# First chunks in three transfers, chunk 1 by terms, last tile scaled by ScalarE

## The chip, the cores and the metric

The kernel runs on one core of a Trainium2 chip. The metric is device time in microseconds of one execution. Engines: TensorE (PE in the rows, its weight load PEld), VectorE (DVE), ScalarE (ACT), GpSimd (POOL) and SyncE (SP), which here only issues transfers.

## The reference

A gate mixes a linear-attention block and a dense block over the same 2048 x 448 input:

```python
qkv = x @ wqkv                       # 16 heads of 28
pq, pk = phi(q), phi(k)              # phi(t) = where(t > 0, t + 1, exp(t)) + 1e-6
kv = einsum("bhsd,bhse->bhde", pk, v); z = pk.sum over s
a = (pq @ kv) / (pq . z + 1e-6) @ wo
h = x @ w1 + b1                      # w1: 448 x 1792
b = relu(h)**2 @ w2 + b2             # w2: 1792 x 448
g = sigmoid((x * gate_w).sum(-1))
return g * a + (1 - g) * b
```

## The kernel before

Every float32 operand is split into a high part in float32r and a low remainder, so a product is three matmuls: high by high, high by low, low by high. ScalarE mostly makes the high parts (`split_hi`, line 63), VectorE the low ones (`split_lo`, line 71).

Tokens go in 4 blocks of 512 (`TB`), hidden features in 14 tiles of 128. The contraction over 448 input features is cut into 4 chunks c = 0 to 3 of 128 rows; chunk 3 holds 64 features twice, so that two matmuls do for it. `up_chunk` (line 218) issues one chunk's two or three terms of one hidden tile, and its argument `only` picks a single term. `hidden` applies bias, relu and square; `down` multiplies by w2 into four accumulators `o_ps`; `finish` (line 275) ends an output tile: `u = o_ps * (1 - g) + part`, where `part` holds what was summed earlier, and a transfer out.

The order on TensorE, VectorE and ScalarE is the order of the code. SyncE's and GpSimd's instructions are placed by a scheduler as early as their waits allow. SyncE's transfers go in turn over eight semaphores, so one also waits for the landing of the one eight places before. Buffers for short-lived data are 15 slots used in turn (`slot`, line 54); a tile that reuses a slot waits until the old one has been read.

The start (lines 173 to 206 and 537 to 560): 14 matmuls on constants run on TensorE (line 177) while the first transfers are on their way. The first two, `xwr`, each bring half the columns of chunk 0 of x beside half of chunk 0 of w1 (128 x 512, 256 KB each). Then come chunks 1 to 3 of x (`xr`) and w1 (`w1r`), 256 KB each, and later weights. For chunk 0 ScalarE makes x's high part and VectorE w1's, half by half. TensorE multiplies the first half of x for hidden tiles 0 and 1, then the second half (line 547), then hidden tiles 2 and 3 over all 512 columns, then the two terms with low parts. Chunks 1 to 3 go tile by tile: all terms of hidden tile 0, then of tile 1, and so on, into the four accumulators `first[0..3]` (`h_ps` in the rows).

The end (lines 765 to 774): the last token tile's result is finished in two column ranges, 0 to 256 and 256 to 448. VectorE does both, one after the other, from the same PSUM tile; SyncE sends out the first, ScalarE's queue the second.

Of the kernel before, what the change touches and what calls it, by code (L numbers as in the profile page):

```python
# [7 lines left out]
F = mybir.dt.float32  # L8
R = mybir.dt.float32r
AF = mybir.ActivationFunctionType  # L10
ALU = mybir.AluOpType
PSUM = bass.MemoryType.PSUM

S, D, FF, H = 2048, 448, 1792, 16
DH = D // H
P = 128
TB = 512
# [10 lines left out]


@with_exitstack  # L30
def gated_mix_kernel(ctx: ExitStack, tc: tile.TileContext, xw, xt, xn, wk, wq, wv, wo, w1a, w1b, w2, b1, b2, gw,
                     hmask, kvmask, halves, out):
    nc = tc.nc
    act, dve, pool, pe, sp = nc.scalar, nc.vector, nc.gpsimd, nc.tensor, nc.sync
# [13 lines left out]
    def bank(name):  # L48
        turn[0] ^= 1
        return ms_p.tile([P, 512], F, name=name, tag=f"ms{turn[0]}")  # L50
# [3 lines left out]
    def slot(shape, dt, name):  # L54
        return work.tile(shape, dt, name=name, tag="s", bufs=NSLOT)

    def load(dst, src):
        sp.dma_start(out=dst, in_=src)
# [4 lines left out]
    def split_hi(eng, hi, src):  # L63
        if eng is act:
            act.activation(hi, src, AF.Copy)  # L65
        elif eng is pool:
            pool.tensor_scalar(hi, src, 1.0, 0.0, op0=ALU.mult, op1=ALU.add)
        else:
            eng.tensor_copy(hi, src)  # L69

    def split_lo(eng, lo, src, hi):
        eng.tensor_tensor(lo, src, f32(hi), op=ALU.subtract)  # L72
# [100 lines left out]
    part = [keep.tile([P, D], F, name=f"part{t}") for t in range(NT)]  # L173
# [8 lines left out]
    dve.memset(side[64:], 1.0)  # L182

    xw_raw = []
    for n in range(2):
        xw_raw.append(slot([P, TB], F, f"xwr{n}"))
        load(xw_raw[n], xw[n])
    for c in range(1, 4):
        load_x(0, c)
        load_w1(0, 0, c)  # L190
# [27 lines left out]
    def up_chunk(ps, b, f, c, only=None):  # L218
        h, fl = divmod(f, NH)
        g, i = divmod(fl, 4)  # L220
        w, cols = w1_s[h, g], slice(i * P, (i + 1) * P)
        xh, xl = xs[b]
        if c < 3:
            terms = [(w[:, c, cols], xh[:, c]), (w[:, c, cols], xl[:, c]), (w[:, 4 + c, cols], xh[:, c])]
        else:
            terms = [(w[:, 3, cols], xh[:, 3]), (w[:, 3, cols], xl[:, 3])]
        for n, (a, m) in enumerate(terms):
            if only in (None, n):
                pe.matmul(ps, a, m, start=(c == 0 and n == 0), stop=(c == 3 and n == 1))  # L229
# [17 lines left out]
    o_ps = {}  # L247
# [24 lines left out]
        for i in range(4):  # L272
            dve.tensor_tensor(part[4 * b + i], o_ps[i][:, :D], b2_s, op=ALU.add)

    def finish(b, i, cols=slice(0, D), eng=sp):
        t = 4 * b + i
        u = slot([P, D], F, f"out{t}_{cols.start}")[:, cols]
        dve.scalar_tensor_tensor(u, o_ps[i][:, cols], gate[:, 1, t:t + 1], part[t][:, cols], op0=ALU.mult,  # L278
                                 op1=ALU.add)
        eng.dma_start(out=out[t * P:(t + 1) * P, cols], in_=u)  # L280


    pend = {}
# [250 lines left out]

    first = [mm_p.tile([P, 512], F, name=f"h_ps0_{f}", tag="mm") if f < 2 else bank(f"h_ps0_{f}") for f in range(4)]
    for c in range(4):
        if c == 0:
            xs[0] = new_x(0)  # L540
            w, (xh, xl) = new_w1(0, 0), [x[:, 0] for x in xs[0]]
            sides = slice(0, TB // 2), slice(TB // 2, TB)
            for n, cols in enumerate(sides):
                split_hi(act, xh[:, cols], xw_raw[n][:, sides[0]])
                split_hi(dve, w[:, 0, cols], xw_raw[n][:, sides[1]])
                for f in range(2):
                    pe.matmul(first[f][:, cols], w[:, 0, f * P:(f + 1) * P], xh[:, cols], start=(n == 0), stop=False)  # L547
            for m, (lo, hi) in enumerate(((xl, xh), (w[:, 4], w[:, 0]))):
                for n, cols in enumerate(sides):
                    split_lo(dve, lo[:, cols], xw_raw[n][:, sides[m]], hi[:, cols])  # L550
        else:
            split_x(0, c)
            split_w1(0, 0, c)
        if c == 0:
            for n in range(3):
                for f in range(0 if n else 2, 4):
                    up_chunk(first[f], 0, f, c, n)
        else:
            for f in range(4):
                up_chunk(first[f], 0, f, c)  # L560
    split_w2(0)
    split_w2(1)
    wk_s = keep.tile([P, 7, D], R, name="wk_s", tag="wkm", bufs=1)
# [53 lines left out]
    for b in range(1, NB):  # L617
        for f in range(NH):
            leave = leaves[b][f]
            run_todo()  # L620
            up(b, f)
            if f == 0:
                down(b - 1, NH - 1)
                half_done(b - 1)
                if b == 1:
                    for c in range(1, 4):
                        todo += gram(0, c)
                        run_todo()
            else:
                down(b, f - 1, leave=leave)  # L630
            if f == 1:
                todo += late_keys
                run_todo()
            if f == 0:
                load_xn(4 * b)
            if f < 4:
                if f < 3:
                    load_xn(4 * b + f + 1)
                if f == 0 and leave:
                    late_keys = keys(4 * b, leave)  # L640
                else:
                    late_keys = []
                    todo += keys(4 * b + f)
            elif f < 6:
                todo += gram(b, f - 4)
            else:
                todo += gram(b, 2)
                run_todo()
                todo += gram(b, 3)
            if b + 1 < NB:  # L650
                if 1 <= f < 5:
                    load_x(b + 1, f - 1)
                if 3 <= f:
                    split_x(b + 1, f - 3)
            if b == 2:
                if f < 4:
                    load_wq(f)
                if 1 <= f < 5:
                    split_wq(f - 1)
                if f == 5:  # L660
                    raw = slot([P, P], F, "hmr")
                    pool.dma_start(out=raw, in_=hmask)
                    split_hi(act, hm, raw)
                    load(half, halves)
            if b == 3:
                if f < 4:
                    load_w1(1, 0, f)
                if f == 4:
                    for c in range(4):
                        split_w1(1, 0, c)  # L670
                if f >= 2:
                    load_w2(NH + f - 2)
                if f >= 3:
                    split_w2(NH + f - 3)
                if f == 5:
                    key_sums()
                if f >= 5:
                    load_kv(2 * f - 10)
                    load_kv(2 * f - 9)
# [87 lines left out]
    for i in range(4):  # L767
# [2 lines left out]
        down(last, NF - 1, [i])  # L770
        if i < 3:
            finish(last, i)
    finish(last, 3, slice(0, 256))
    finish(last, 3, slice(256, D), act)


# [52 lines left out]
```

## Time and profile before

| what | value |
|---|---|
| median of 3 runs | 435.39 us (435.03 to 435.49) |
| profiled execution, its own time | 435.59 us |
| its span, first to last instruction | 433.8 us |
| TensorE busy | 429.5 us (99%) |
| VectorE, ScalarE, GpSimd busy | 283.7, 174.5, 72.1 us |
| chain that ended last: TensorE's share | 98% |

The profiled execution lies 0.20 us above the median and 0.10 above the highest of the three runs. 1.8 us of its time lie outside the span. Times in rows count from the start of the span.

### The profile page before, as it was taken

To read this page: it belongs to the slowest core of one execution; us is meant where nothing else is said; L and a number is where in the kernel's file an instruction comes from. 1 tells how busy PE (TensorE), PEld (TensorE's weight loads), DVE (VectorE), ACT (ScalarE), POOL (GpSimd) and SP (SyncE) were. 2 spreads that over 40 slices of the span, in tenths; PEclk is the share of its full clock that TensorE was granted. 3 is DMA by queue.
4 is the path that set the end of the run, shared out by engine and by line. 5 is a ranking of instruction groups with operands and counts; after the bars stand their busy time and mean duration, and the time that the engine had idled before them with its cause. 6 is when DMAs were issued, how large, how long until landed. Compare 5 with 4: busy or idle time off the path is not lost.

```text
span 433.8 us, 5561 instructions
## 1 busy us (share of the span) xinstructions
PE 429.5 (99%) x2052; PEld 381.4 (88%) x2052; DVE 283.7 (65%) x462; ACT 174.5 (40%) x302; POOL 72.1 (17%) x93
## 2 busy tenths in 40 slices
PE   9999999999999999999999999999999999999996
PEld 7898999898989899898898888988888888888986
DVE  5899518843499437784449777887653967457624
ACT  6865324421346122453145443444433434233421
POOL 0045006500065002540010441000100001000000
PEclk9999999999999999999999999999999999999999
DMA  7741302020221211223244321130101301002002
GB/s 282 240 134 51 109 0 69 27 68 1 70 82 65 72 45 48 65 58 111 63 118 134 69 65 38 61 122 0 26 0 48 136 0 26 0 0 86 0 2 85
DMA packets 18347, 29.00 MB, mean 67 GB/s; under 512 B 2896, under 2 KB 12672, under 8 KB 18320
## 3 DMA queue, kind: packets, MB, share of 16 engines
q1 hardware_dynamic: 16416, 26.35, 19.5%
q0 software_dynamic: 1760, 2.20, 2.3%
q8 instruction: 16, 0.26, 0.3%
q14 instruction: 11, 0.09, 0.1%
q10 hardware_dynamic: 144, 0.10, 0.1%
HBM read 22.31 MB, written 3.67 MB: 60 GB/s over the span
## 4 chain that ended last, share of the span: by engine, by line
PE 98%; DMA 1%; DVE 0%; ACT 0%; DVEq 0%; issue 0%
PE h_ps L229 32%; PE o_ps L254 31%; PE q_ps L84 8%; PE k_ps L254 8%; PE a_ps L84 8%; PE g_ps L84 8%; PE kv_ps L404 1%; DMA xwr<-in_xw 1%; PE m_ps L84 1%; PE d_ps L84 0%; PE h_ps L547 0%; PE z_ps L398 0%; DVE out L278 0%; ACT xh L65 0%; DVEq L825 0%
## 5 line engine op out<-in xcount | busy, mean ns | idle before, releaser
L254 PE MATMUL o_ps<-w,hh 128*128 128x448 f32 x448 | 128.6, 362 | 0.0
L229 PE MATMUL h_ps<-xh,w 128*128 128x512 f32 x390 | 124.8, 391 | 0.0
L254 PEld LDWEIGHTS o_ps<-w,hh 128*128 128x128 f32 x448 | 84.0, 187 | 7.7
L229 PE MATMUL h_ps<-xl,w 128*128 128x512 f32 x224 | 87.0, 391 | 0.0
L229 PEld LDWEIGHTS h_ps<-xh,w 128*128 128x128 f32 x390 | 73.4, 188 | 14.1
L254 PE MATMUL o_ps<-w,hl 128*128 128x448 f32 x224 | 81.2, 362 | 0.0
L233 ACT ACTIVATE hr<-h_ps,b_s 128x512 f32<-128x512 f32 x56 | 38.1, 680 | 86.1 <-PE h_ps L229 80.8
L69 DVE CAST hh<-hr 128x512 fp32r<-128x512 f32 x56 | 23.5, 420 | 61.8 <-ACT hr L234 61.7
L229 PEld LDWEIGHTS h_ps<-xl,w 128*128 128x128 f32 x224 | 42.4, 189 | 8.0
L254 PEld LDWEIGHTS o_ps<-w,hl 128*128 128x128 f32 x224 | 42.0, 188 | 3.7
L72 DVE TENSOR_TENSOR hl<-hr,hh 128x512 fp32r<-128x512 f32 x56 | 39.7, 709 | 3.3
L72 POOL TENSOR_TENSOR nl<-xnr,nh 128x384 fp32r<-128x384 f32 x16 | 17.2, 1076 | 119.0 <-ACT nh L65 118.9
L234 ACT ACTIVATE hr<-hr 128x512 f32<-128x512 f32 x56 | 35.4, 632 | 1.8
L84 PE MATMUL q_ps<-xh,wq_s 128*128 128x512 f32 x100 | 33.1, 390 | 0.0
L84 PE MATMUL a_ps<-m_s,qh 128*128 128x448 f32 x112 | 32.7, 362 | 0.0
L254 PE MATMUL k_ps<-wk_s,xh 128*128 128x448 f32 x112 | 32.7, 361 | 0.0
L474 POOL DMA_DIRECT2D qr<-qv x16 | 7.9, 503 | 124.3 <-ACT qv L471 94.5
L72 DVE TENSOR_TENSOR pl<-r,ph 128x448 fp32r<-128x448 f32 x16 | 23.7, 1479 | 0.0
L327 POOL TENSOR_TENSOR ksum<-ksum,r 128x448 f32<-128x448 f32 x15 | 23.3, 1555 | 1.1 <-DVE r L289 1.1
L84 PE MATMUL q_ps<-xl,wq_s 128*128 128x512 f32 x60 | 23.4, 389 | 0.0
L254 PE MATMUL k_ps<-wk_s,xl 128*128 128x448 f32 x64 | 23.2, 363 | 0.0
L84 PE MATMUL a_ps<-m_s,ql 128*128 128x448 f32 x64 | 23.2, 362 | 0.0
(111 smaller groups left out, 565.8 us busy)
## 6 DMA issues: line engine op xcount, KB each, us to landing
xr<-in_xt SPq DMA_DIRECT2D x27, 256.0 KB, 2.7
xnr<-in_xn SPq DMA_DIRECT2D x16, 224.0 KB, 2.5
out<-out SPq DMA_DIRECT2D x15, 224.0 KB, 1.9
w2r<-in_w SPq DMA_DIRECT2D x14, 224.0 KB, 2.7
w1r<-in_w1a SPq DMA_DIRECT2D x7, 256.0 KB, 2.7
w1r<-in_w1b SPq DMA_DIRECT2D x8, 192.0 KB, 3.3
m_s<-m POOLq DMA_DIRECT2D x12, 112.0 KB, 2.5
wqr<-in_wq SPq DMA_DIRECT2D x4, 256.0 KB, 2.7
```

Of the source, the lines that this page charges most:

```text
L69: eng.tensor_copy(hi, src)
L72: eng.tensor_tensor(lo, src, f32(hi), op=ALU.subtract)
L84: pe.matmul(out_ps, a, b, start=(i == 0), stop=(i == n - 1))
L229: pe.matmul(ps, a, m, start=(c == 0 and n == 0), stop=(c == 3 and n == 1))
L233: act.activation(r, ps, AF.Relu, bias=b1_s[:, f:f + 1])
L234: act.activation(r, r, AF.Square)
L254: pe.matmul(ps, a, m, start=start, stop=stop)
L327: pool.tensor_tensor(ksum, ksum, p, op=ALU.add)
L404: pe.matmul(kv_ps[:JE, js], wv_s[c][:, js], gsum[c][:, js], start=(c == 0), stop=(c == 3))
L474: pool.dma_start(out=r[p + 16:p + 32], in_=v[p:p + 16])
```

## The change

It has four parts. (1) Chunk 0 comes in three transfers in place of two: half the columns of x beside w1's hidden tile 0 (128 x 384, 192 KB), the other half beside hidden tile 1 (192 KB), and w1's hidden tiles 2 and 3 (128 x 256, 128 KB). VectorE now makes x's high part and ScalarE w1's. (2) Chunk 1's products, like chunk 0's, are issued term by term over the four hidden tiles. (3) The small table `half` is loaded by GpSimd in place of SyncE. (4) For the last token tile ScalarE scales columns 256 to 448 into SBUF, VectorE ends columns 0 to 256 as before and then adds `part` to ScalarE's result. The host arranges the same bytes in other arrays.

```diff
-    for n in range(2):
-        xw_raw.append(slot([P, TB], F, f"xwr{n}"))
-        load(xw_raw[n], xw[n])
+    for n, src in enumerate((xw0, xw1, w1c)):
+        xw_raw.append(slot([P, src.shape[1]], F, f"xwr{n}"))
+        load(xw_raw[n], src)
...
-            sides = slice(0, TB // 2), slice(TB // 2, TB)
-            for n, cols in enumerate(sides):
-                split_hi(act, xh[:, cols], xw_raw[n][:, sides[0]])
-                split_hi(dve, w[:, 0, cols], xw_raw[n][:, sides[1]])
-                for f in range(2):
-                    pe.matmul(first[f][:, cols], w[:, 0, f * P:(f + 1) * P], xh[:, cols], start=(n == 0), stop=False)
-            for m, (lo, hi) in enumerate(((xl, xh), (w[:, 4], w[:, 0]))):
-                for n, cols in enumerate(sides):
-                    split_lo(dve, lo[:, cols], xw_raw[n][:, sides[m]], hi[:, cols])
+            hx = TB // 2
+            xcols, wcols = (slice(0, hx), slice(hx, TB)), (slice(0, P), slice(P, 2 * P), slice(2 * P, TB))
+            for n in range(2):
+                split_hi(dve, xh[:, xcols[n]], xw_raw[n][:, :hx])
+                split_hi(act, w[:, 0, wcols[n]], xw_raw[n][:, hx:])
+            split_hi(act, w[:, 0, wcols[2]], xw_raw[2])
+            for f, n in ((0, 0), (0, 1), (1, 0), (1, 1)):
+                pe.matmul(first[f][:, xcols[n]], w[:, 0, wcols[f]], xh[:, xcols[n]], start=(n == 0), stop=False)
...
-        if c == 0:
-            for n in range(3):
-                for f in range(0 if n else 2, 4):
-                    up_chunk(first[f], 0, f, c, n)
-        else:
-            for f in range(4):
-                up_chunk(first[f], 0, f, c)
+        for n in range(3) if c < 2 else (None,):
+            for f in range(2 if (c, n) == (0, 0) else 0, 4):
+                up_chunk(first[f], 0, f, c, n)
...
-                    load(half, halves)
+                    pool.dma_start(out=half, in_=halves)
...
-    finish(last, 3, slice(0, 256))
-    finish(last, 3, slice(256, D), act)
+
+    t, ps = 4 * last + 3, o_ps[3]
+    u = [slot([P, D], F, f"out{t}_{n}") for n in range(2)]
+    cols = slice(0, 256), slice(256, D)
+    act.activation(u[1][:, cols[1]], ps[:, cols[1]], AF.Copy, scale=gate[:, 1, t:t + 1])
+    dve.scalar_tensor_tensor(u[0][:, cols[0]], ps[:, cols[0]], gate[:, 1, t:t + 1], part[t][:, cols[0]],
+                             op0=ALU.mult, op1=ALU.add)
+    dve.tensor_tensor(u[1][:, cols[1]], u[1][:, cols[1]], part[t][:, cols[1]], op=ALU.add)
+    for n, queue in enumerate((sp, act)):
+        queue.dma_start(out=out[t * P:(t + 1) * P, cols[n]], in_=u[n][:, cols[n]])
```

On TensorE the first real products stood so before, where `h_ps_0` to `h_ps_3` are the accumulators of hidden tiles 0 to 3, and a name in brackets is what an instruction waits for:

```order
L547 MATMUL h_ps_0_165<-xh_169,w_00_171 128x256 [waits DVE_49,Activation_49]
L547 MATMUL h_ps_1_166<-xh_169,w_00_171 128x256
L547 MATMUL h_ps_0_165<-xh_169,w_00_171 128x256 [waits Activation_49]
L547 MATMUL h_ps_1_166<-xh_169,w_00_171 128x256
L229 MATMUL h_ps_2_167<-xh_169,w_00_171 128x512 [waits DVE_49]
L229 MATMUL h_ps_3_168<-xh_169,w_00_171 128x512
```

And now:

```order
L549 MATMUL h_ps_0_167<-xh_171,w_00_173 128x256 [waits DVE_49,Activation_49]
L549 MATMUL h_ps_0_167<-xh_171,w_00_173 128x256 [waits DVE_49]
L549 MATMUL h_ps_1_168<-xh_171,w_00_173 128x256 [waits Activation_49]
L549 MATMUL h_ps_1_168<-xh_171,w_00_173 128x256
L229 MATMUL h_ps_2_169<-xh_171,w_00_173 128x512 [waits Activation_49]
L229 MATMUL h_ps_3_170<-xh_171,w_00_173 128x512
```

Hidden tile 0 takes both halves of x before hidden tile 1 begins, and tile 2 waits for ScalarE's split of the third transfer where it waited for VectorE's split of the second.

On SyncE's queue the first transfers stood so before (`xwr` chunk 0, `xr` and `w1r` the later chunks):

```order
L58 DMA xwr_110<-in_xw 128x512
L58 DMA xwr_112<-in_xw 128x512
L58 DMA xr_1_114<-in_xt 128x512
L58 DMA w1r_116<-in_w1a 128x512
L58 DMA xr_2_118<-in_xt 128x512
```

And now:

```order
L58 DMA xwr_110<-in_xw 128x384
L58 DMA xwr_112<-in_xw 128x384
L58 DMA xwr_114<-in_w1c 128x256
L58 DMA xr_1_116<-in_xt 128x512
L58 DMA w1r_118<-in_w1a 128x512
L58 DMA xr_2_120<-in_xt 128x512
```

Every later transfer of the start stands one issue further back, behind the same bytes. With `half` gone from the queue the places match again from `w2r` on; on GpSimd's queue `half` now stands first of all, ahead of the first `ksum` copy.

On VectorE the last instructions were these, where `o_ps_7_3` is the accumulator of the last token tile:

```order
L525 SCALAR_TENSOR_TENSOR part_86<-part_86,gate,u_3759 128x448 [waits Activation_49]
L278 SCALAR_TENSOR_TENSOR out_0_3774<-o_ps_7_0_3522,gate,part_83 128x448 [waits DMAHW1_49,PE_49]
L278 SCALAR_TENSOR_TENSOR out_0_3780<-o_ps_7_1_3523,gate,part_84 128x448 [waits PE_49]
L278 SCALAR_TENSOR_TENSOR out_0_3786<-o_ps_7_2_3524,gate,part_85 128x448 [waits PE_49]
L278 SCALAR_TENSOR_TENSOR out_0_3795<-o_ps_7_3_3525,gate,part_86 128x256 [waits DVE_49,PE_49]
L278 SCALAR_TENSOR_TENSOR out_256_3798<-o_ps_7_3_3525,gate,part_86 128x192
```

And now:

```order
L524 SCALAR_TENSOR_TENSOR part_86<-part_86,gate,u_3763 128x448 [waits Activation_49]
L278 SCALAR_TENSOR_TENSOR out_3778<-o_ps_7_0_3526,gate,part_83 128x448 [waits DMAHW1_49,PE_49]
L278 SCALAR_TENSOR_TENSOR out_3784<-o_ps_7_1_3527,gate,part_84 128x448 [waits PE_49]
L278 SCALAR_TENSOR_TENSOR out_3790<-o_ps_7_2_3528,gate,part_85 128x448 [waits PE_49]
L777 SCALAR_TENSOR_TENSOR out_0_3799<-o_ps_7_3_3529,gate,part_86 128x256 [waits DVE_49,Activation_49]
L779 TENSOR_TENSOR out_1_3800<-out_1_3800,part_86 128x192
```

The 256-column instruction, which waited for TensorE, now waits for ScalarE: ScalarE's only instruction after the `u` that `part_86` has already waited for is the new scaling of the same `o_ps_7_3` (line 776).

## Rows read from the trace of the kernel before

**Rows 1.** The page's part 1: busy us, share of the span, instructions.
```profile
PE 429.5 (99%) x2052; PEld 381.4 (88%) x2052; DVE 283.7 (65%) x462; ACT 174.5 (40%) x302; POOL 72.1 (17%) x93
```

**Rows 2.** Chain of work, stretch 0 to 19: start us, us, what.
```profile
0.74 2.75 DMA xwr<-in_xw
...
5.37 10.20 PE h_ps L229 x42
```

**Rows 3.** Timeline of 0 to 24: start us, us, instruction, [idle before, ended by].
```profile
0.78 3.15 PE L177 MATMUL warm_ps<-const-bfloat16-1.0 128*128 128x256 bf16 x14 [0.78 <-PEq L821]
...
1.64 0.43 SPq L58 DMA_DIRECT2D xr<-in_xt  x1
...
3.51 0.42 ACT L65 ACTIVATE xh<-xwr 128x256 fp32r<-128x256 f32 x1 [1.49 <-DMA xwr<-in_xw]
3.51 0.29 DVE L69 CAST w<-xwr 128x256 fp32r<-128x256 f32 x1 [2.40 <-DMA xwr<-in_xw]
...
3.98 1.39 PE L547 MATMUL h_ps<-xh,w 128*128 128x256 f32 x4
...
4.11 0.42 ACT L65 ACTIVATE xh<-xwr 128x256 fp32r<-128x256 f32 x1 [0.18 <-DMA xwr<-in_xw]
...
5.17 1.05 PE L229 MATMUL h_ps<-xh,w 128*128 128x512 f32 x2
...
5.96 0.63 ACT L65 ACTIVATE xh<-xr 128x512 fp32r<-128x512 f32 x1 [1.44 <-DMA xr<-in_xt]
6.02 1.38 PE L229 MATMUL h_ps<-xl,w 128*128 128x512 f32 x4
...
6.66 0.63 ACT L65 ACTIVATE w<-w1r 128x512 fp32r<-128x512 f32 x1
...
7.24 1.31 PE L229 MATMUL h_ps<-xh,w 128*128 128x512 f32 x5
...
7.32 0.69 DVE L72 TENSOR_TENSOR w<-w1r,w 128x512 fp32r<-128x512 f32 x1
...
19.74 0.82 POOL L325 COPY ksum<-r 128x448 f32<-128x448 f32 x1 [18.86 <-DVE r L289]
```

**Rows 4.** TensorE by stretches: length, busy (instructions), granted clock, DMA share, GB/s.
```profile
5.17:6.45 1.28, 1.28 (x5) 1.00 1.03 378
...
16.00:100.00 84.00, 84.00 (x407) 1.00 0.24 71
```

**Rows 5.** All engines' busy time, stretch 2.5 to 3.5; GB/s last.
```profile
2.50:3.50 1.00, 1.00 (x6) 0.68 (x5) 0.00 (x0) 0.00 (x0) 0.00 (x0) 1.00 1.00 387
```

**Rows 6.** Timeline of the end, 427 to 434.
```profile
429.98 0.37 PE L254 MATMUL o_ps<-w,hl 128*128 128x448 f32 x1
430.39 0.81 DVE L278 SCALAR_TENSOR_TENSOR out<-o_ps,gate,part 128x256 f32<-128x256 f32 x2 [0.52 <-PE o_ps L254]
431.23 0.37 ACTq L280 DMA_DIRECT2D out<-out  x1
```

**Rows 7.** Groups by shape, VectorE and ScalarE: busy us, mean ns, idle before.
```profile
L278 DVE SCALAR_TENSOR_TENSOR out<-o_ps,gate,part 128x256 f32<-128x256 f32 x1 | 0.5, 485 | 0.5 <-PE o_ps L254 0.5
L278 DVE SCALAR_TENSOR_TENSOR out<-o_ps,gate,part 128x192 f32<-128x192 f32 x1 | 0.4, 408 | 0.0
...
L524 ACT ACTIVATE u<-a_ps,gate 128x448 f32<-128x448 f32 x16 | 10.2, 635 | 28.3 <-PE a_ps L84 28.3
...
L65 ACT ACTIVATE hm<-hmr 128x128 fp32r<-128x128 f32 x1 | 0.3, 296 | 0.0
```

**Rows 8.** Who waited for whom: us in total, times, longest.
```profile
DVE r L288 <- ACT e L287: 10.1, 9, 1.9
```

**Rows 9.** Timeline of 17 to 20: both readers of `k_ps`.
```profile
17.81 0.55 ACT L287 ACTIVATE e<-k_ps 128x448 f32<-128x448 f32 x1 [0.97 <-PE k_ps L254]
...
18.39 0.62 DVE L288 TENSOR_SCALAR r<-k_ps 128x448 f32<-128x448 f32 x1 [0.36 <-ACT e L287]
```

**Rows 10.** The page's part 3, SyncE's queue: packets, MB, share of 16 engines.
```profile
q1 hardware_dynamic: 16416, 26.35, 19.5%
```

More of the change, by code (lines that the diff above doesn't have):

```diff
@@ L30, in gated_mix_kernel @@
 @with_exitstack
-def gated_mix_kernel(ctx: ExitStack, tc: tile.TileContext, xw, xt, xn, wk, wq, wv, wo, w1a, w1b, w2, b1, b2, gw,
+def gated_mix_kernel(ctx: ExitStack, tc: tile.TileContext, xw0, xw1, w1c, xt, xn, wk, wq, wv, wo, w1a, w1b, w2, b1, b2, gw,
                      hmask, kvmask, halves, out):
@@ L273, in half_done, with finish @@
             dve.tensor_tensor(part[4 * b + i], o_ps[i][:, :D], b2_s, op=ALU.add)
-    def finish(b, i, cols=slice(0, D), eng=sp):
+    def finish(b, i):
         t = 4 * b + i
[L277 to L280, printed above, removed]
+        u = slot([P, D], F, f"out{t}")
+        dve.scalar_tensor_tensor(u, o_ps[i][:, :D], gate[:, 1, t:t + 1], part[t], op0=ALU.mult, op1=ALU.add)
+        load(out[t * P:(t + 1) * P], u)
     pend = {}
@@ L541, in gated_mix_kernel @@
             w, (xh, xl) = new_w1(0, 0), [x[:, 0] for x in xs[0]]
-            sides = slice(0, TB // 2), slice(TB // 2, TB)
-            for n, cols in enumerate(sides):
-                split_hi(act, xh[:, cols], xw_raw[n][:, sides[0]])
-                split_hi(dve, w[:, 0, cols], xw_raw[n][:, sides[1]])
-                for f in range(2):
-                    pe.matmul(first[f][:, cols], w[:, 0, f * P:(f + 1) * P], xh[:, cols], start=(n == 0), stop=False)
-            for m, (lo, hi) in enumerate(((xl, xh), (w[:, 4], w[:, 0]))):
-                for n, cols in enumerate(sides):
-                    split_lo(dve, lo[:, cols], xw_raw[n][:, sides[m]], hi[:, cols])
+            hx = TB // 2
[6 more added lines that the diff above has]
+                pe.matmul(first[f][:, xcols[n]], w[:, 0, wcols[f]], xh[:, xcols[n]], start=(n == 0), stop=False)
+            for n in range(2):
+                split_lo(dve, xl[:, xcols[n]], xw_raw[n][:, :hx], xh[:, xcols[n]])
+            for n, raw in enumerate((xw_raw[0][:, hx:], xw_raw[1][:, hx:], xw_raw[2])):
+                split_lo(dve, w[:, 4, wcols[n]], raw, w[:, 0, wcols[n]])
         else:
@@ L801 @@
     a = {
-        "xw": np.stack([np.concatenate([t[:, n * TB // 2:(n + 1) * TB // 2] for t in (xt[0, 0], w1[0, 0])], axis=1)
-                        for n in range(2)]),
+        "xw0": np.concatenate([xt[0, 0, :, :TB // 2], w1[0, 0, :, :P]], axis=1),
+        "xw1": np.concatenate([xt[0, 0, :, TB // 2:], w1[0, 0, :, P:2 * P]], axis=1),
+        "w1c": w1[0, 0, :, 2 * P:TB],
         "xt": xt,
```

## The prediction

> **What bounds the kernel now.** I read the page's busy shares first: TensorE works 429.5 of 433.8 us [rows 1]. Next the chain of waits: it starts with the first transfer, 2.75 us from 0.74, and from 5.37 runs along TensorE [rows 2]. The stretches then show TensorE without a gap: 84.00 us busy of 84.00 between 16 and 100 [rows 4]. So time can be gained or lost only where TensorE is not yet, or no longer, the limit: in the first 8 us and after the last matmul. For those I read the timelines [rows 3, 6], and last who waits for whom [rows 8]. The change touches just these two places; between them the order on TensorE is the same.
>
> At the start the reader is to see two things. First the spacing: two 512-column products from 5.17 to 6.02 are 0.43 us each, five from 7.24 on stand 0.23 apart, since the fifth starts at 7.24 + 4 x 0.23 = 8.16 and chunk 1 with it [rows 3]. [...] The four products from 6.02 take 1.22 us: about two and a half at 0.43 and the rest at 0.23, so the level changes near 6.6. [...] The first real product starts at 3.98, and four of 0.21 us take until 5.17, which is 1.19 for 0.85 [rows 3]. Idle in all: 0.26 + 0.34 = 0.60 us. That is everything that a better start can close, and it lies at the low clock.
>
> **The start, part by part.** The first transfer shrinks from 256 to 192 KB. At the 387 GB/s of that stretch [rows 5] 64 KB are 0.17 us, so it lands at 3.49 - 0.17 = 3.32. VectorE's cast of 256 columns takes 0.29 [rows 3]; ScalarE's of 128 columns about 0.30 [rows 7]. The operands stand at 3.63, before the warm-up ends: the first product moves from 3.98 to about 3.72. The second transfer landed at 4.09, just ahead of ScalarE's cast at 4.11 [rows 3]; there are 128 KB less up to its end, 0.33 us, so 3.76, and its casts end at 4.07. From there three products of 0.21 bring TensorE to about 4.75. Hidden tiles 2 and 3 need the third transfer. By bytes it lands where the second did, 4.09; by issue it may be one issue of 0.43 later [rows 3], 4.5. ScalarE needs 0.42 for its 256 columns: ready at 4.53 or 4.95. So tile 2 begins at 4.75 or, at the late end, 5.0, in place of 5.17: 0.42 or about 0.15 us sooner, and nothing if this transfer straggles as chunk 1's x does, which arrives at 5.94, 4.3 us after its issue at 1.64 [rows 3].
>
> What that is worth hangs on the clock. If it rises at the same 6.6, the 0.42 us are columns done at 0.43 that would have been done at 0.23 later: 0.42 x 0.23 / 0.43 = 0.22. If it rises that much sooner, all 0.42 stay. Bounds 0 and 0.42; I take 0.28, nearer to the unmoved clock.
>
> Chunk 1 by terms gains nothing that this trace shows: the five products at equal 0.23 run from chunk 0 into chunk 1 without a pause [rows 3]. It is cover. ScalarE ends w1's high part at 6.66 + 0.63 = 7.29, VectorE its low part at 7.32 + 0.69 = 8.01. TensorE will now come to chunk 1 at about 7.8. Tile by tile the low part would be wanted two products later, 8.25; by terms eight later, 9.6. Without the new order the earlier start would have 0.25 us of slack there.
>
> Every later transfer stands one issue (0.43) further back, behind the same bytes. Chunk 1's x waited far longer than that for its turn, so I cost the shift at nothing; if it came through whole, ScalarE's high part would end at 7.72, just before 7.8. Later weights wait for the landing of the same data as before.
>
> `half`, 1 KB in 128 rows, goes out on GpSimd's queue right at the start, beside the first transfers. GpSimd has nothing else until 19.74 [rows 3]. On the engines it costs between nothing and 128 mean packets: 19.5% of 433.8 us on 16 engines for 16416 packets is 0.08 us each, eight per engine, 0.66 us [rows 10]. Rows of 8 bytes are far below the mean; I take 0.05, inside the rounding above.
>
> **The end.** TensorE's last product starts at 429.98 and is out at 430.36. VectorE's two instructions start at 430.39 and take 0.81 together, ScalarE's queue issues the last transfer at 431.23 [rows 6]. The new code looks as if ScalarE and VectorE work side by side. They don't: the 256-column instruction now waits for ScalarE's scaling, by the order shown above. The trace has this wait: the first step of the keys has two readers of one PSUM tile, of which neither needs the other's result, and VectorE starts at 18.39, 0.03 after ScalarE ends at 17.81 + 0.55 [rows 9]; there are nine such waits [rows 8].
>
> [...]
>
> ScalarE's time for 192 columns isn't in the trace. Its 448 columns with a scale per row take 0.635 [rows 7], and plain casts of 256 and 512 columns 0.42 and 0.63 [rows 3], 0.82 ns a column: 0.635 - 256 x 0.82 ns = 0.42. Bounds: 0.30 (the 128-column cast) and 0.635 [rows 7]. I take 0.42, plus 0.03 for the hand-over. VectorE then needs its 256 columns, 485 ns, of which the next instruction overlaps a part, and an add of 192 columns where it had 408 ns for scale and add [rows 7]; I take 0.37 for the add, 0.04 less, with 0.29 (the 256-column cast) and 0.41 as bounds. Sum: +0.42 + 0.03 - 0.04 = +0.41; from the ends of both, +0.21 to +0.67. ScalarE's queue issues the last transfer that much later, and nothing behind it changes.
>
> **Sum.** -0.28 + 0.41 = +0.13 us. On the profiled execution's 435.59 that is 435.72. It lies 0.20 above the median of the runs; set against that median the forecast is 435.5 us. A measurement of this kernel can tell 0.2%, 0.87 us, from no change, so this is no change.
>
> **Rivals.** (a) The clock rises much sooner, because TensorE is no longer idle between warm-up and first product: faster. A product at the low level costs 0.20 us more than at the high one, so each microsecond by which the rise comes sooner gives 0.20 / 0.43 = 0.47 us. Two and a half microseconds sooner, at 4.1, and the holes closed whole: 0.41 - 0.60 x 0.5 - 2.5 x 0.47 = -1.07, 434.3; beyond 0.2% from 2.1 us sooner on. For it: the holes lie just before the rise, and the three runs spread over 0.46 us, as they would if the rise came at different times. Against it: 2.9 us of unbroken warm-up didn't bring the rise here. [...] Chance 0.15, of which 0.11 beyond 0.2%.
>
> (b) The start gives nothing, because the third transfer lands late or ScalarE, which now makes three casts in a row, becomes the limit: 435.39 + 0.41 = 435.8. For it: chunk 1's x, which stood third in the queue, was the straggler. Chance 0.18, no change.
>
> (c) Chunk 1 arrives too late: slower. Its w1 high part has some 0.5 us in hand (7.29 against 7.8). One issue, 0.43, and `half`'s upper bound of 0.66 would push it to 8.4; it decides from 7.8 on, microsecond for microsecond. That is 0.6 of new wait, and `half` at that price also moves the first product to 3.32 + 0.66 + 0.34 = 4.32, 0.34 late: 435.39 + 0.41 + 0.6 + 0.34 x 0.5 = 436.6. Against it: few bytes, and the transfers wait for bytes, not for issues. Chance 0.10, of which 0.08 beyond 0.2%.
>
> (d) The end does run side by side, so that only the start counts: 435.39 - 0.28 - 0.04 = 435.1. The wait in the order speaks against it. Chance 0.05, no change.
>
> **How the numbers follow.** The forecast itself has 0.52: 435.5, with bounds -0.42 + 0.21 and 0 + 0.67 it lies in 435.2 to 436.1. The three runs lie up to 0.36 below their median, and (a) reaches 434.3; for eight times in ten I take 434.7 to 436.0. Faster by over 0.2%: 0.11 from (a). Slower: 0.08 from (c). Within: the rest, 0.81.
>
> **What the profile after would show.** Right: the first product near 3.7, tile 2's first product near 4.75, no gap on entry to chunk 1; at the end ScalarE's 128x192 instruction straight after the last matmul, VectorE's 256 columns after it, the last issue some 0.4 us further from the last matmul than now. Wrong: VectorE starting beside ScalarE; 0.23 us spacing well before 6.6; a gap on TensorE near 8; the third transfer's cast later than 5.

## The result, and the profile after

The changed kernel takes 436.46 us (median of 9 executions, 436.15 to 438.14), the kernel before, run beside it on the same chip, 435.40 (9 executions, 435.03 to 435.63): a ratio of 1.0030, interval 1.0018 to 1.0043. It is slower by 1.06 us. Forecast was 435.5, range 434.7 to 436.0, no change: wrong, and outside the range. Two of the nine executions, 437.73 and 438.14, lie over a microsecond above the other seven; before had none so far out.

The profiled execution took 436.38 us against 435.59 before. The page's part 1 of the kernel after, against [rows 1]:

```profile
PE 428.9 (99%) x2052; PEld 381.0 (88%) x2052; DVE 283.8 (65%) x463; ACT 175.1 (40%) x304; POOL 72.6 (17%) x94
```

TensorE is busy 0.6 us less and the span is 0.8 us longer (434.6 for 433.8). So the work on TensorE didn't grow; it waits 1.4 us more. The timeline of the start says where, read against [rows 3] (start us, us, instruction, idle before and what ended it):

```profile
1.65 0.43 SPq L58 DMA_DIRECT2D xwr<-in_w1c  x1
...
3.20 0.31 ACT L65 ACTIVATE w<-xwr 128x128 fp32r<-128x128 f32 x1 [1.18 <-DMA xwr<-in_xw]
...
3.64 1.38 PE L549 MATMUL h_ps<-xh,w 128*128 128x256 f32 x4
3.66 0.31 ACT L65 ACTIVATE w<-xwr 128x128 fp32r<-128x128 f32 x1 [0.15 <-DMA xwr<-in_xw]
...
5.56 0.42 ACT L65 ACTIVATE w<-xwr 128x256 fp32r<-128x256 f32 x1 [1.59 <-DMA xwr<-in_w1c]
6.01 0.42 DVE L72 TENSOR_TENSOR w<-xwr,w 128x256 fp32r<-128x256 f32 x1 [0.98 <-ACT w L65]
6.03 0.73 PE L229 MATMUL h_ps<-xh,w 128*128 128x512 f32 x2 [1.01 <-ACT w L65]
...
6.60 1.07 PE L229 MATMUL h_ps<-xl,w 128*128 128x512 f32 x4
...
7.51 1.98 PE L229 MATMUL h_ps<-xh,w 128*128 128x512 f32 x8
```

The first product starts at 3.64, 0.34 us sooner than before, and the second half's casts at 3.66, 0.45 sooner: both a little better than forecast. But the third transfer, issued at 1.65, is there only at about 5.55, 3.9 us later. ScalarE stands 1.59 us before its cast, and TensorE 1.01 us by the row: tile 2 begins at 6.03, before it was 5.17, forecast was 4.75 to 5.0.

The last row shows eight products 0.23 us apart from 7.51, four of chunk 0 and four of chunk 1, so chunk 1 starts at 7.51 + 4 x 0.23 = 8.42 and TensorE does not stop there. Before it started at 8.16: 0.26 us lost, not the whole 0.86 by which tile 2 is late. The rest came back from the clock. The trace's record of the granted clock begins, at 1.00 of full speed, at 4.95 us here and at 6.64 before, and the spacing of the products agrees: here the ten of 512 columns from 6.03 on stand 0.23 apart, but for the second, 0.34 behind the first, while before three and part of a fourth after 5.17 took 0.43 each.

The end, against [rows 6]:

```profile
430.35 0.37 PE L254 MATMUL o_ps<-w,hl 128*128 128x448 f32 x1
430.75 0.42 ACT L776 ACTIVATE out<-o_ps,gate 128x192 f32<-128x192 f32 x1 [4.17 <-PE o_ps L254]
431.21 0.48 DVE L777 SCALAR_TENSOR_TENSOR out<-o_ps,gate,part 128x256 f32<-128x256 f32 x1 [0.97 <-ACT out L776]
431.61 0.35 DVE L779 TENSOR_TENSOR out<-out,part 128x192 f32<-128x192 f32 x1
...
431.99 0.37 ACTq L781 DMA_DIRECT2D out<-out  x1
```

VectorE's 256 columns wait for ScalarE's scaling, though they don't use it. From the start of the last matmul to the last issue 1.64 us pass, before 1.25: the end costs 0.39 us. The last matmul itself starts 0.37 us later than before, of which 0.26 were there at chunk 1. So the two profiled executions, 0.8 us apart, divide about evenly between start and end.

### The profile page after: what moved, and what is told of

Same layout as the page of the kernel before. It is cut to its first block, busy times and chain, and to the rows that moved or that the text cites. A ratio compares the mean times of both kernels' runs of the same rounds, so it can differ in the third digit from the quotient of the medians.

```text
span 434.6 us, 5568 instructions
## 1 busy us (share of the span) xinstructions
PE 428.9 (99%) x2052; PEld 381.0 (88%) x2052; DVE 283.8 (65%) x463; ACT 175.1 (40%) x304; POOL 72.6 (17%) x94
## 4 chain that ended last, share of the span: by engine, by line
PE 98%; DMA 1%; ACT 0%; SPq 0%; DVE 0%; issue 0%; DVEq 0%
PE h_ps L229 32%; PE o_ps L254 31%; PE q_ps L84 8%; PE a_ps L84 8%; PE g_ps L84 8%; PE k_ps L254 8%; DMA xwr<-in_w1c 1%; PE kv_ps L403 1%; PE m_ps L84 1%; PE d_ps L84 0%; SPq L58 0%; PE z_ps L397 0%; DVE out L777 0%; ACT out L776 0%; ACT w L65 0%
```

## The experiments

Each was timed beside the kernel before on one chip; its medians in these sessions were 435.33 to 435.49, and of the 92 executions in these sessions the highest was 436.56.

**Start and end apart.** The end alone (kernel before, last tile's code as in the change):

```diff
-    finish(last, 3, slice(0, 256))
-    finish(last, 3, slice(256, D), act)
+    act.activation(u[1][:, cols[1]], ps[:, cols[1]], AF.Copy, scale=gate[:, 1, t:t + 1])
...
```

> The kernel before with the new end alone (ScalarE scales columns 256 to 448, VectorE waits for it). Theory: the end costs 0.40 us by the two profiles (last matmul to end of span 3.83 before, 4.23 after), so 435.8 us, and VectorE's 256-column instruction starts 0.45 us after ScalarE's. Rival: the end's cost is hidden or belongs to the profile alone, 435.4 us.

435.69 us, ratio 1.0006 (0.9997 to 1.0014). The median moved by 0.30, which the timing alone does not tell from nothing. The profile measures the end by itself: from the last matmul's start to the last issue 431.43 - 429.79 = 1.64, as in the changed kernel.

```profile
429.79 0.37 PE L254 MATMUL o_ps<-w,hl 128*128 128x448 f32 x1
430.20 0.42 ACT L775 ACTIVATE out<-o_ps,gate 128x192 f32<-128x192 f32 x1 [4.17 <-PE o_ps L254]
430.65 0.48 DVE L776 SCALAR_TENSOR_TENSOR out<-o_ps,gate,part 128x256 f32<-128x256 f32 x1 [0.97 <-ACT out L775]
431.05 0.35 DVE L778 TENSOR_TENSOR out<-out,part 128x192 f32<-128x192 f32 x1
...
431.43 0.37 ACTq L780 DMA_DIRECT2D out<-out  x1
```

This run also showed that the moment of the clock's rise belongs to the execution rather than to the kernel: its start is that of before, yet the record of the granted clock begins at 3.85 us, against 6.64 in the profile of before.

The start alone (the changed kernel with `finish` of before at the end):

> The changed kernel with the old end. Theory: what is left of the loss, 1.06 - 0.40 = 0.66 us, sits in the start, where hidden tiles 2 and 3 wait for the third transfer: 436.05 us, with the third transfer's cast near 5.5 us and the first 512-column product near 6.0. Rival: the start is even (the gap there is made good by the earlier first product and the clock), and the loss came from the end alone: 435.4 us.

435.94 us, ratio 1.0020 (1.0008 to 1.0032): the start, forecast to win 0.28, loses 0.55. Three of twelve executions lie at 437.63 to 437.72, the other nine at 435.42 to 435.99. The profile, one of the nine, has the same hole, with the cast and tile 2 where the theory had them (5.5 and 6.0):

```profile
5.46 0.42 ACT L65 ACTIVATE w<-xwr 128x256 fp32r<-128x256 f32 x1 [1.51 <-DMA xwr<-in_w1c]
...
5.92 0.73 PE L229 MATMUL h_ps<-xh,w 128*128 128x512 f32 x2 [1.07 <-ACT w L65]
```

**Does the small table hold the third transfer up?** The changed kernel with `half` on SyncE again:

```diff
-                    pool.dma_start(out=half, in_=halves)
+                    load(half, halves)
```

> The changed kernel with the table half loaded by SyncE again. Theory P (place): the third transfer is late whatever runs beside it, as chunk 1's x was when it stood third: cast of the third transfer between 5.3 and 6.0 us, time 436.4 us as the changed kernel. Theory H (half): the small transfer on GpSimd's queue, whose pieces run from 3.1 to 4.9 us, holds up the engines that carry the third: without it the cast starts at 4.1 to 4.6 us, and the time is 435.6 to 435.8 us, the end's 0.40 remaining less some gain.

437.05 us, ratio 1.0041 (1.0028 to 1.0054): not better. The third transfer's cast starts at 5.10 rather than 5.56: between the ranges of the two theories (4.1 to 4.6 and 5.3 to 6.0), nearer to theory P's. The hole is still 0.56 us. In this execution the products stay 0.43 apart until 9.45 and the whole took 438.07.

```profile
5.10 0.42 ACT L65 ACTIVATE w<-xwr 128x256 fp32r<-128x256 f32 x1 [1.14 <-DMA xwr<-in_w1c]
...
5.57 1.22 PE L229 MATMUL h_ps<-xh,w 128*128 128x512 f32 x2 [0.56 <-ACT w L65]
...
6.59 1.91 PE L229 MATMUL h_ps<-xl,w 128*128 128x512 f32 x4
```

**Two transfers in place of three** (start alone; tiles 2 and 3 of w1 come with the second, which grows to 128 x 640 and is called `pair` in the rows):

```diff
-        "xw1": np.concatenate([xt[0, 0, :, TB // 2:], w1[0, 0, :, P:2 * P]], axis=1),
-        "w1c": w1[0, 0, :, 2 * P:TB],
+        "xw1": np.concatenate([xt[0, 0, :, TB // 2:], w1[0, 0, :, P:TB]], axis=1),
...
```

> The changed kernel with the old end and with w1's hidden tiles 2 and 3 in the second transfer (128 x 640) in place of a third one; half stays on GpSimd's queue. Theory P: with nothing of chunk 0 in the third place the second lands near 4.1 us, the first 512-column product starts at 4.9 to 5.1, and chunk 1's x, now third, arrives near 6 without hurting: 435.2 us, at most 0.2 under the kernel before. Theory H: half's pieces now fall on the second transfer's end and on chunk 1's x: first 512-column product at 5.5 or later, 435.8 us.

436.34 us, ratio 1.0019 (1.0005 to 1.0033), in two groups: six executions at 434.82 to 435.90, six at 436.78 to 437.67. The profile, of the upper group, shows the second transfer cast at 4.39; the hole has moved ahead of the second half's products (0.49 us by the row), and the products stay 0.43 apart to 9.85.

```profile
4.40 0.29 DVE L69 CAST xh<-pair 128x256 fp32r<-128x256 f32 x1 [0.83 <-DMA pair<-in_xw]
...
4.74 1.01 PE L553 MATMUL h_ps<-xh,w 128*128 128x256 f32 x3 [0.49 <-DVE xh L69]
```

So w1's last two tiles need not be late, but bringing them sooner makes a hole elsewhere. The first 512-column product starts at 5.55, at theory H's mark (5.5 or later) and not at theory P's (4.9 to 5.1), but behind that hole and at 0.43 a product, so this profile doesn't show that `half` is the reason. And the profiled execution, of the upper group, is one in which the clock rises late. What is the hole's part in that?

**The hole filled with useful work.** The start alone, with chunk 0's order changed: all three terms of tiles 0 and 1, whose operands the first two transfers bring, ahead of tiles 2 and 3.

```diff
-        for n in range(3) if c < 2 else (None,):
-            for f in range(2 if (c, n) == (0, 0) else 0, 4):
-                up_chunk(first[f], 0, f, c, n)
+        for fs in (((0, 1), (2, 3)) if c == 0 else (range(4),)):
+            for n in range(3) if c < 2 else (None,):
+                for f in fs:
+                    if (c, n) != (0, 0) or f >= 2:
+                        up_chunk(first[f], 0, f, c, n)
```

> The changed start (three transfers, casts per piece, chunk 1 by terms) with the end of before, and one more move: in chunk 0 all three terms of tiles 0 and 1 go ahead of tiles 2 and 3, so that four products of 512 columns, whose operands the first two transfers bring, stand where TensorE waited for the third transfer (4.82 to 6.03 us in the changed kernel). Theory A (the start lost its time to the wait for the third transfer, and to a clock that rises late when it rises beside that hole): no hole of over 0.1 us between the first product at 3.6 and chunk 1, first row of tile 2 at 6.2 to 6.7 at the slow clock; 0.34 us of the earlier begin and the 0.6 us of holes of before are won back, half of that where the clock rises at the same moment: 434.5 to 435.0, and no executions at 437 and above. Theory B (the pieces cost by themselves: smaller products, more casts, a busy queue): no better than the start alone, 435.9, whatever the order.

435.25 us, ratio 0.9997 (0.9988 to 1.0006), eleven executions from 435.00 to 436.19, none higher. The loss of the start is gone, as theory A had it and theory B not; the gain of 0.4 or more over before that A named is not there. The profile (its clock record begins at 3.95) says why:

```profile
3.58 1.04 PE L550 MATMUL h_ps<-xh,w 128*128 128x256 f32 x4
...
4.67 0.73 PE L229 MATMUL h_ps<-xl,w 128*128 128x512 f32 x2
...
5.21 0.42 ACT L65 ACTIVATE w<-xwr 128x256 fp32r<-128x256 f32 x1 [1.26 <-DMA xwr<-in_w1c]
5.23 1.19 PE L229 MATMUL h_ps<-xh,w 128*128 128x512 f32 x4
...
6.77 0.63 ACT L65 ACTIVATE w<-w1r 128x512 fp32r<-128x512 f32 x1
...
7.45 0.76 PEld L229 LDWEIGHTS h_ps<-xh,w 128*128 128x128 f32 x4 [0.53 <-ACT w L65]
```

The third transfer is cast at 5.21 and the four products of tiles 0 and 1 stand in front of it. TensorE now reaches chunk 1 early and waits there for w1's second chunk, cast from 6.77 on. The next transfer in the row has become the bound.

**The hole filled with work that gives nothing.** The start alone, with six products on constants after the first four:

```diff
+            for _ in range(6):
+                pe.matmul(first[2][:, :256], warm[:, :P], warm, start=True, stop=True)
```

> The changed start with the end of before, and six products of 256 columns on constants (like the warm-up's; into the bank of tile 2, which its first product then overwrites) between the four products of tiles 0 and 1 and the wait for the third transfer: the hole of 1.0 us is filled with work that gives nothing. Theory A1 (a hole in TensorE's work beside the rise of the clock is what lets the slow stretch last to 9.5 us in some executions, 437.6 to 437.7): the median is at or under that of the start alone (435.9) and no execution lies above 437. Theory A2 (the moment of the rise is not tied to the hole): three in twelve executions stay at 437.6, and the median is at 435.9 to 436.1.

435.93 us, ratio 1.0013 (1.0004 to 1.0022), eleven executions from 435.15 to 436.21. The median is that of the start alone, which waits in the same place, but the group at 437.6 is gone, as A1 had it. In the profile, the lowest of the eleven, the third transfer is cast as early as 4.88:

```profile
4.62 0.84 PE L552 MATMUL h_ps<-const-bfloat16-1.0 128*128 128x256 bf16 x6
4.88 0.42 ACT L65 ACTIVATE w<-xwr 128x256 fp32r<-128x256 f32 x1 [0.94 <-DMA xwr<-in_w1c]
...
5.35 0.73 PE L229 MATMUL h_ps<-xh,w 128*128 128x512 f32 x2
```

**Is it the short rows of the third transfer?** The start alone, that transfer widened to 128 x 512 (2 KB rows, the right half not used); one execution:

```diff
-        "w1c": w1[0, 0, :, 2 * P:TB],
+        "w1c": np.concatenate([w1[0, 0, :, 2 * P:TB], w1[0, 0, :, :2 * P]], axis=1),
...
```

> The changed start with the end of before; the third transfer widened from 128x256 to 128x512 (2 KB rows as in the kernel before, 256 KB; the right half is brought and not used). One look at when it lands. Theory P (whatever stands third in the queue lands 3.9 to 4.3 us after its issue, because the queue slows between 3.2 and 4.8 us): it lands at 5.5 to 6.2, the rate of the queue still falls under 250 GB/s between 3.2 and 4.8, and the first product of tile 2 begins at 6.0 to 6.6. Theory R (the short rows of 1 KB are what goes slowly, packets of 0.5 to 0.9 us): no packets of over 0.4 us in that stretch, landing by 4.9, tile 2 at 5.4.

It is cast at 5.98, TensorE takes up tile 2 at 6.45:

```profile
5.98 0.42 ACT L65 ACTIVATE w<-xwr 128x256 fp32r<-128x256 f32 x1 [2.01 <-DMA xwr<-in_w1c]
...
6.45 1.22 PE L229 MATMUL h_ps<-xh,w 128*128 128x512 f32 x2 [1.43 <-ACT w L65]
```

So rows of 1 KB are not needed to make it late: it lands 4.3 us after its issue, as long as chunk 1's x takes in third place before [rows 3]. But this rests on one of its sixteen parts in one execution: fifteen are in by 4.88, the last at 5.96. Theory P's other half failed: the rate fell under 250 GB/s only between 3.2 and 3.6 and was 292 from 3.6 to 4.0, where the changed kernel has 52. So the short rows are not cleared: they remain a candidate for the slow stretch, though theory R's other mark, no packet over 0.4 us, failed too (the longest up to 4.8 took 0.66). The clock record begins at 12.5 us and this execution took 439.09, the longest of all, behind the longest hole.

**The third transfer on another queue.** The start alone, the third transfer issued by ScalarE at 0.74:

```diff
-        load(xw_raw[n], src)
+        (sp, sp, act)[n].dma_start(out=xw_raw[n], in_=src)
```

> The changed start with the end of before, the third transfer issued from ScalarE's queue at about 0.7 us rather than third on SyncE's at 1.65; the same bytes and the same order of work. Theory P (its place behind two others on one queue makes it late): it lands by 4.5, the first two 0.2 to 0.4 us later than now (2.9 and 3.5) as they share the rate with it; tile 2 begins behind the four first products with a hole under 0.3 us, and the median falls from 435.9 to 435.3 or less. Theory S (between 3.2 and 4.8 us every transfer goes slowly, whichever queue it is on): the rate in that stretch still falls under 200 GB/s; if part of the third transfer is still under way by then it lands at 5.0 or later and the median stays at 435.8 or more.

435.49 us, ratio 1.0002 (0.9992 to 1.0012): the loss of the start is gone this way too, with nothing won; the median lies between the two theories' marks (435.3 and 435.8). The third transfer's last part lands at 3.86 us, and the first product moves to 4.16, as its own transfer now lands at 3.69 rather than 3.18:

```profile
0.74 0.41 ACTq L187 DMA_DIRECT2D xwr<-in_w1c  x1
...
3.72 0.31 ACT L65 ACTIVATE w<-xwr 128x128 fp32r<-128x128 f32 x1 [1.26 <-DMA xwr<-in_xw]
...
4.16 1.49 PE L550 MATMUL h_ps<-xh,w 128*128 128x256 f32 x4 [0.24 <-ACT w L65]
```

Its profiled execution is the one of ten above 436.2 (437.23; clock record from 9.79), so the row is not the median's. In it the rate falls under 200 GB/s later than in the changed kernel, at 4.4 to 5.2. So bringing the third transfer out of third place makes it early, as P had it; queue and time of issue changed together here and are not told apart. That there is a stretch in which everything crawls, as S has it, fits too, but not at a fixed time.

**Chunk 1 by terms alone** (kernel before with that one edit):

```diff
-            for f in range(4):
-                up_chunk(first[f], 0, f, c)
+        for n in range(3) if c < 2 else (None,):
+            for f in range(2 if (c, n) == (0, 0) else 0, 4):
+                up_chunk(first[f], 0, f, c, n)
```

> The kernel before, with chunk 1 by terms as in the changed kernel and nothing else. My theory: with the clock's rise at 6.6 as in the trace of before, chunk 1's operands are there in time and nothing is won (435.4); where the clock rises early, as in the run with the new end alone, whose TensorE stood 0.72 us on entry to chunk 1, up to 0.7 is won: median 435.0 to 435.4. Rival: the order by terms reaches the later tiles' first terms before the operands they need and costs 0.1 to 0.3: 435.5 to 435.7.

435.61 us, ratio 1.0004 (0.9993 to 1.0015): no difference that can be told; the median lies in the rival's range, but the interval holds both theories. One of the eleven executions took 437.18. Where the order could help, the profile of the end alone shows it: with the clock up at 3.85, TensorE tile by tile comes to chunk 1 by 7.2 and loses 0.7 us over the next products.

```profile
7.55 0.50 PE L229 MATMUL h_ps<-xh,w 128*128 128x512 f32 x1 [0.17 <-ACT w L65]
7.89 0.40 PE L229 MATMUL h_ps<-xl,w 128*128 128x512 f32 x1
8.28 0.73 PE L229 MATMUL h_ps<-xh,w 128*128 128x512 f32 x2
```

By terms, with the clock up at 5.11, the profile of this run goes into chunk 1 without a stop, four products of chunk 0 and four of chunk 1 in 1.84 us; but chunk 1's w1 was there 0.3 us sooner as well (cast at 6.56, in the end alone at 6.87).

```profile
6.46 2.00 PE L229 MATMUL h_ps<-xh,w 128*128 128x512 f32 x8
```

**The next bound split.** The reordered start, with w1's second chunk cast in two halves by ScalarE and VectorE:

```diff
+            for eng, cols in ((act, slice(0, 256)), (dve, slice(256, 512))):
+                split_hi(eng, w[:, 1, cols], raw[:, cols])
...
```

> The start with tiles 0 and 1 of chunk 0 first (its run: 435.25, TensorE from 3.58, clock up at 3.95, and then 0.38 us of waiting on entry to chunk 1, at 6.96 to 7.45 and 7.45 to 7.79, behind the 0.63 us cast of chunk 1's w1, which landed at 6.75); here that cast is done in two halves, the left by ScalarE, the right by VectorE, side by side. Theory C (with the hole gone, chunk 1's w1 and its cast bound the start): chunk 1 begins about 0.45 us after the landing and waits once, 0.2 to 0.35 us less in all: 434.9 to 435.05. Rival: the landing alone decides, or the lower half of x, pushed behind on VectorE, waits instead: 435.2 to 435.4.

435.40 us, ratio 0.9996 (0.9987 to 1.0005). The median is the rival's, at the edge of its range. In the profile the cast does start on both engines at once and chunk 1 begins 0.47 us later, as theory C had it, but all of it at 7.19 rather than 6.77, because this time the data came then. In this execution the landing decides.

```profile
7.19 0.29 DVE L69 CAST w<-w1r 128x256 fp32r<-128x256 f32 x1 [1.00 <-DMA w1r<-in_w1a]
7.19 0.42 ACT L65 ACTIVATE w<-w1r 128x256 fp32r<-128x256 f32 x1
...
7.66 1.19 PE L229 MATMUL h_ps<-xh,w 128*128 128x512 f32 x4 [0.22 <-ACT w L65]
```

**The changed kernel with the order of chunk 0 mended**, its own end kept (the edit is that of the reordered start):

> The changed kernel whole, its new end too, with one edit: in chunk 0 all three terms of tiles 0 and 1 stand ahead of tiles 2 and 3. Theory A (the loss of the start is the wait for the third transfer with what it does to the clock, and the end costs its 0.4 us whatever the start does): 435.25 of this start with the old end, plus 0.4: 435.6 to 435.7, ratio to before near 1.0006, and no executions above 437. Rival (start and end do not add up; the changed kernel's loss has another part): 436.0 or more.

435.91 us, ratio 1.0011 (1.0002 to 1.0020), eleven executions from 435.51 to 436.84. One reorder takes away 0.55 of the 1.06 us and every execution above 437. It is 0.2 to 0.3 above what theory A named and under the rival's 436.0; against the reordered start with the old end (435.25, another session) the new end makes 0.66, where the traces give it 0.39. The difference is of the size by which medians of before move between sessions plus the scatter within one. What remains is not told apart here. The profile shows that the four useful products don't cover every landing: the third transfer is cast at 5.54, and four products from 5.26 on take 1.32 us where four at 0.23 would take 0.92.

```profile
5.26 1.49 PE L229 MATMUL h_ps<-xh,w 128*128 128x512 f32 x4
...
5.54 0.42 ACT L65 ACTIVATE w<-xwr 128x256 fp32r<-128x256 f32 x1 [1.56 <-DMA xwr<-in_w1c]
...
6.58 0.62 PE L229 MATMUL h_ps<-xl,w 128*128 128x512 f32 x2
...
429.49 0.37 PE L254 MATMUL o_ps<-w,hl 128*128 128x448 f32 x1
...
431.13 0.37 ACTq L783 DMA_DIRECT2D out<-out  x1
```

No version beats the kernel before by more than the interval.

## Why the prediction was wrong

**The end was right.** Forecast +0.41, measured 0.39 in the traces of all three kernels that have it (1.64 us from the last matmul to the last issue in each, 1.25 before); by the timing alone, +0.30 with an interval that holds zero. ScalarE's 192 columns take 0.42 (taken: 0.42), VectorE starts 0.46 us after ScalarE did, and the add takes 0.35 with what it overlaps. The wait was read from two readers of one PSUM tile [rows 9], and it is there, so rival (d) is out. In the changed kernel VectorE starts at 431.21, 0.04 us after ScalarE ends at 430.75 + 0.42; in [rows 9] it was 0.03.

**The step that failed is the landing of the third transfer**, "By bytes it lands where the second did, 4.09; by issue it may be one issue of 0.43 later [rows 3], 4.5", and with it the bound of zero: "nothing if this transfer straggles as chunk 1's x does". It straggled so: 3.9 us from issue in the changed kernel, 4.3 widened, where 4.3 for the third in the queue stood in [rows 3]. The sum from that row is 1.65 + 4.3 + 0.42 = 6.37 for tile 2, a loss of up to 1.2 us against 5.17. It was named and then set to zero, though the row says more than zero. The start was to be -0.28, with 0 as its worst; it is +0.55 alone. Rival (b) had the mechanism (a late third transfer) with this same wrong price. The start's 0.55 and the end's 0.39 make 0.94 of the 1.06 us; the rest is within the scatter of such medians. Two of the prediction's signs of being wrong appeared: the cast later than 5, and 0.23 us spacing well before 6.6.

Two readings of the trace of before were off, without deciding the outcome. The four products from 6.02 in 1.22 us are one and a half at 0.43 and two and a half at 0.23, not the other way round; the rise near 6.6 stands. And of the 0.60 us of idle (0.26 from 3.72, 0.21 after the start of the last warm-up product at 3.51, to 3.98, and 0.34 among the first products) the 0.34 did not close with the earlier data: the four first products take 1.39 before and 1.38 after. Before, they start at 3.98, 4.36, 4.58 and 4.96, 0.38 instead of 0.21 behind the first and the third, and ahead of the third the cast of the second half was done at 4.53.

Why a late third transfer costs more than in the kernel before: there the third to arrive was chunk 1's x, wanted only after the whole of chunk 0, and it cost no wait. The change put in third place data that TensorE wants as its fifth product. Filling that place with four products whose data is there (435.25), or getting the data out of third place (435.49), each brings the start back to the time of before.

**What was not foreseen is the clock's spread.** That products at 0.43 and at 0.23 show two levels of the clock was the prediction's reading of their spacing. The traces agree with it: in the kernel before the step from 0.43 to 0.23 lies between 6.45 and 6.77, and the clock's record begins at 6.64; in the changed kernel 256 columns still take 0.22 at 4.39 and 512 take 0.23 from 6.37 on, and the record begins at 4.95. The forecast took the rise at 6.6 us for fixed and gave a sooner one 0.15. In the profiles it came at 3.5 to 5.1 us in eight kernels, at 6.64 in the kernel before, and at 9.45 to 12.5 in four. The four with the late rise took 437.23 to 439.09. In all four TensorE had stood before that, 0.24 to 1.43 us at one place by the rows shown above. The profiles alone don't show the link, though: those of the changed kernel and of the start alone have holes of 1.01 and 1.07 us, but their clock had risen as the hole began (4.95) or before it (4.56), and with the hole filled by useful products it rose at 3.5 to 3.95, ahead of the place that was filled. The times point to it: of 27 timed executions with the hole behind the first four products (changed kernel, start alone, `half` on SyncE) seven took 437.6 or more, of 44 with that hole filled or shortened, by useful products or by products on constants, none did. That filling the hole removes the upper group is well supported, not proven: these two sets ran in different sessions, on different chips as far as the record names them, and beside the filled ones only the widened transfer ran with the hole (one execution, 439.09). Nor is this hole the only way there: the kernel before with chunk 1 by terms has one execution at 437.18, the third transfer on ScalarE's queue one at 437.23. How the chip decides is not shown. The changed kernel's profile had the early rise and still lost 0.26 at chunk 1, so hole and late rise are two costs: about 0.5 us in the nine lower executions of the start alone, and 1.3 to 1.8 more where an execution of it or of the changed kernel lies in the upper group.

Rival (a) had the right sign for the clock (a sooner rise does come, also in kernels with the old start), but not the gain: where the clock is early TensorE catches up with the transfers, and waits for chunk 1's w1 (7.45 in the reordered start). By these profiles that is also why no better start won anything measurable. Rival (c), chunk 1 too late, did not happen in the changed kernel: there is no gap at 8.42. But that transfers wait for bytes and not for issues, which was held against it, is not shown: it fits the stretches at 378 and 387 GB/s [rows 4, 5] and not the third transfer, whose 128 KB took 3.9 us with the rate down to 52.

Chunk 1 by terms costs nothing that can be told, as forecast. The shift of the later transfers costs nothing in the changed kernel, where chunk 1's x and w1 are cast 0.25 and 0.18 us later than before and TensorE does not stop for them. `half` at 0.05 can't be confirmed: without it on GpSimd's queue the third transfer was cast 0.46 us sooner in one execution, which is within the scatter of such landings (with it, five profiles have the cast at 5.21 to 5.56 and the filled one at 4.88).

## What to carry to other kernels

A transfer's landing is read from the place in the queue that it will have, at the row of what stood there before, and not from its bytes alone: in third place at the start the profiles have 3.2 to 3.9 us from issue for 128 KB and 4.2 to 4.9 for 256 KB, where the prediction took 2.4 to 2.9 for the 128 KB. If an argument names a row that makes a step a loss, the bound is that loss and not zero. When pieces arrive in turn, put every product whose operands are there ahead of the first one that needs the next piece; here that one reorder undid the start's whole loss with the old end (435.25 against 435.33), and 0.55 of the changed kernel's 1.06.

## What the runs showed of the hardware

- In the changed kernel the transfers move far less around 3.2 to 4.8 us than just before. By stretches (length; busy time of TensorE, weight loads, VectorE, ScalarE, GpSimd; granted clock, DMA share, GB/s): the engines count as 0.8 to 0.9 busy while the rate is 52 to 195 GB/s, and 376 before that.

```profile
2.40:2.80 0.40, 0.40 (x4) 0.29 (x2) 0.00 (x0) 0.00 (x0) 0.00 (x0) 1.00 1.02 376
...
3.20:3.60 0.40, 0.40 (x4) 0.17 (x2) 0.29 (x1) 0.31 (x1) 0.00 (x0) 1.00 0.77 132
3.60:4.00 0.40, 0.40 (x3) 0.29 (x1) 0.34 (x2) 0.31 (x1) 0.00 (x0) 1.00 0.79 52
4.00:4.40 0.40, 0.40 (x3) 0.39 (x3) 0.40 (x2) 0.00 (x0) 0.00 (x0) 1.00 0.89 174
4.40:4.80 0.40, 0.40 (x3) 0.33 (x2) 0.40 (x3) 0.00 (x0) 0.00 (x0) 1.00 0.79 195
```

  From 3.6 to 4.0 the seven profiles with the 128 x 256 transfer third on SyncE's queue have 52 to 190 GB/s, the other six 210 to 335; the kernel before is at 210 with a share of 0.63, the widened transfer at 292, two transfers in place of three at 250. At that time, then, the slow stretch goes with that transfer in that place. But the widened one falls to 80 from 3.2 to 3.6, and the third transfer on ScalarE's queue to 118 from 4.4 to 4.8, so no one cause is shown. `half` is neither needed nor enough: with it on SyncE the four stretches from 3.2 still show 175, 72, 77 and 230, and with it on GpSimd but two transfers the least is 250. What the cause is stays open.
- The column of the granted clock prints 1.00 in these rows, though the clock's record begins only at 4.95 us and the warm-up's products of 256 columns stand 0.21 us apart up to 3.5 us, almost what 512 columns take later (0.23): ahead of the first record the spacing has to be read.
- A transfer lands when the last of its sixteen parts does; in the widened one that was 1.08 us behind the fifteenth, in the changed kernel's third 0.02 (5.54 against 5.52), and its cast starts at 5.56.
- The product behind one that has waited comes late as well: in the changed kernel tile 2's product at 6.03 is followed at 6.37, 0.34 us later, and the next ones stand 0.23 apart; at the low level, before, 4.36 follows 3.98 by 0.38 where 0.21 would do. So in these rows a wait costs 0.1 to 0.2 us more than the idle time. Why is not shown.
